# A pre-norm linear-attention and FFN kernel on one core: three loads on another queue, the FFN weights' loads placed between the rows of reciprocal loads instead of among them, and a hand-written order laid out anew

## The chip, the core and the metric

The kernel runs on one core of a Trainium2 chip. A time is that of one execution on the device, in microseconds (us). Engine names: PE is TensorE (matmuls; PEld its weight loads), DVE is VectorE, ACT is ScalarE, POOL is GpSimd, SP is SyncE, which here issues nearly all DMAs.

## The reference

All data are bf16. One batch of 2048 tokens, width 512, FFN width 1792.

```python
def _A_ref(x, wqkv, wo):                      # 32 heads of 16
    q, k, v = qkv[0], qkv[1], qkv[2]          # x @ wqkv, split by head
    phi = lambda t: jnp.where(t > 0, t + 1, jnp.exp(t)) + 1e-6
    pq, pk = phi(q), phi(k)
    kv = jnp.einsum("bhsd,bhse->bhde", pk, v)
    z = jnp.einsum("bhsd->bhd", pk)
    num = jnp.einsum("bhqd,bhde->bhqe", pq, kv)
    den = jnp.einsum("bhqd,bhd->bhq", pq, z)[..., None] + 1e-6
    o = num / den
    return o.transpose(0, 2, 1, 3).reshape(B, S, D) @ wo

h = x + _A_ref(_layernorm(x), A_wqkv, A_wo)
h2 = h + jnp.maximum(_layernorm(h) @ B_w1, 0) @ B_w2
```

## The kernel before

The 2048 tokens are 16 tiles of 128 rows, in 4 chunks of 4 tiles. The whole program is one list of words, `ORDER`. A word such as `K.7.3` calls `op_K(7, 3)`, and the words are emitted from first to last (L540 to L542). Each engine runs its own instructions in the order of its words, and waits where a word needs another engine's result, a DMA's data, or a buffer that is still being read. So the order between words of different engines means nothing, but the order within one engine, and within SP's queue, means everything. Numbers behind a name are tiles, chunks, rows and PSUM banks (there are 8 banks, all written by hand); the last number of a `T`, `K`, `Q`, `h`, `p` or `f` word without a split is the bank.

**Loads.** `lx` (L213, SP) and `ax` (L216, ACT's queue) load tiles of x: `lx.4.2` loads tiles 4 and 5. `lk`, `lq`, `lv`, `lo`, `l1`, `l2` (L219, SP) load the weights of keys, queries, values, attention output, and the FFN's w1 and w2. `l1` and `l2` come in two halves of 0.9 MB each.

**Attention, part 1, by tile.** `warm` runs matmuls on zeros. `S`, `A` (L233, L234, DVE): mean and variance; `R` (L239, ACT): reciprocal deviation; `N` (L247, DVE): normalized tile. The normalized tile is transposed by `T` (PE, L272) with `E` (ACT, L282) for tiles 0 to 4, by `X` (DMA transpose, L293, issued by SP) for the others. `K` (L301) gives the keys of a tile, `Q` (L309) the queries of a chunk, transposed. phi is built by `F` and `U` (ACT: exp and relu), `M` and `D` (DVE: min and add), and with a q ahead of the name (`qF`, `qU`, `qM`, `qD`) for queries. `G` (L353) sums phi(k)^T times the normalized rows in banks 4 to 7; `za`, `zf`, `zhi`, `zlo`, `z` sum phi(k).

**Attention, part 2.** `gA`, `gD` (L391, L394) evict G; `kv`, `kx`, `m` (L399, L407, L411) and `mA` or `mD` (ACT L414, DVE L417) form one 512x512 matrix that holds kv and wo. `d4` (L425) gives the denominators of a chunk, `dl4` and `dx4` (ACT) their reciprocals by Ln and Exp. `wb` (L453) writes these 128x512 values to DRAM; eight `rb` words (L456) read them back, each row set broadcast over 16 partitions, into `rr`, of which there is one for all chunks. `dm` (L469, DVE) multiplies phi(q) by `rr` into `pqs`; `h` (L478, PE) multiplies by the matrix, a tile at a time, and `hD` (L484, DVE) adds x.

**FFN.** `s`, `a` (L235, L236), `n` (DVE, L255) or `nA` (ACT, L261), and a transpose `x` (L294, by SP) or `t` and `v` (PE, DVE) prepare a tile; `r` (ACT) gives the reciprocal deviation of four tiles. `p` (L493; `ph` for half a chunk, L502) is the first FFN matmul of a chunk, 14 row blocks; two blocks at a time are evicted with relu by `pA` (ACT, L508) or `pD` (DVE, L513). `f` (L522) is the second, by tile, in two runs of 7 matmuls; `fo` (DVE, L530) scales and adds h, `fd` (L537, SP) stores. Tile 15 is done in three pieces of 256, 128 and 128 columns.

Two facts that the steps below use: the words `rb.1.*` of the eight rows of chunk 1 have `l2.7.7` between them in SP's queue, and `wb.0` is followed by `l1.0.2` before the eight `rb.0.*`.

Of the kernel before, what the change touches and what calls it, by code (L numbers as in the profile page):

```python
# [43 lines left out]
pD.1.2.2 n.8 a.14 fd.1 s.12 p.1.5.1 p.1.4.0 pA.1.0.2 fo.2 hD.15 s.15 n.9 pD.1.4.2 a.12 p.1.6.4 p.1.8.2 p.1.7.5
pD.1.6.2 x.10 p.1.10.6 p.1.9.3 p.1.12.4 p.1.11.7 pA.1.8.2 r.4.4 f.5.2.0.7 p.1.13.5 pD.1.12.2 fd.0 x.9 x.8
p.2.10.3 p.2.1.1 p.2.0.0 fd.3 fd.2 p.2.12.4 p.2.13.5 pA.2.0.2 pA.2.12.2 nA.12 pD.1.10.2 a.15 h.13.6 hD.13 n.15
f.7.0.0.7 s.13 a.13 p.2.3.7 p.2.11.4 f.7.0.7.7 pD.2.10.2 f.5.2.7.7 fo.5 nA.14 x.14 nA.13 p.2.2.6 pD.2.2.2 fo.7
f.4.4.0.7 f.6.7.0.7 f.6.7.7.7 p.2.4.5 x.15 p.2.8.0 p.2.5.6 pA.2.4.2 fo.6 x.12 x.13 p.3.7.3 p.2.9.1 f.4.4.7.7
# [524 lines left out]
```

## Time and profile before

| what | value |
|---|---|
| median of 3 runs | 170.41 us (170.07 to 170.49) |
| the profiled execution's own time | 169.75 us |
| its span, first to last instruction | 168.03 us |
| granted TensorE clock | 1.000 |
| last landing of a store | 167.09 us in the span |
| DMA, mean | 95 GB/s, 16.01 MB |

In a line of a timeline the columns are start, duration (both us), engine, line, operation, output<-inputs, count, and in brackets the engine's idle time before it with what ended it. In the chain of work that ended last, they are start, duration and what. In a group, busy time, mean duration in ns, and idle time before. In the page's second part each character is one of 40 slices of 4.2 us, in tenths of busy time. DMA issue lines have the count, KB of one, and the median us from issue to landing. "Matmul, start to start" is the distance between the starts of two neighbours in the trace, since busy times of matmuls overlap.

### The profile page before, as it was taken

The page shows a single profiled execution, that of the slowest core. Times are in us where ns is not written, and L with a number is a line of the kernel's source. Part 1 is how long each engine was busy: PE and PEld are TensorE (multiplying, and loading weights), DVE is VectorE, ACT ScalarE, POOL GpSimd, SP SyncE. Part 2 cuts the span into 40 slices and gives each one's busy share as a digit, 9 for nine tenths or more (in the row PEclk, how much of TensorE's full clock was granted, in tenths as well). Part 3 has the DMA queues.
Part 4 walks back from the last instruction along what each step waited for, and adds up shares of the span by engine and source line. Part 5 has one row for each costly group of instructions (what it writes and reads, how often), then busy time and mean ns, then how long its engine had stood idle before and what let it go on. Part 6 is the DMA issues. An engine that isn't in the chain of part 4 may idle for free.

```text
...
## 1 busy us (share of the span) xinstructions
PE 163.1 (97%) x924; PEld 79.6 (47%) x924; DVE 98.5 (59%) x198; ACT 67.3 (40%) x104; POOL 4.7 (3%) x21
## 2 busy tenths in 40 slices
PE   7899999999999998999999999999999999999993
...
DVE  2999999941659876428799880544415170043133
...
PEclk9999999999999999999999999999999999999999
...
DMA packets 25003, 16.01 MB, mean 95 GB/s; under 512 B 15008, under 2 KB 23968, under 8 KB 24992
## 3 DMA queue, kind: packets, MB, share of 16 engines
...
q8 instruction: 7, 0.11, 0.3%
q14 instruction: 4, 0.03, 0.1%
...
## 4 chain that ended last, share of the span: by engine, by line
PE 85%; DVE 5%; DMA 5%; SPq 2%; issue 1%; DVEq 0%
PE bk L522 29%; PE bk L493 24%; PE bk L301 8%; PE bk L353 8%; PE bk L478 7%; PE bk L309 6%; DMA rr<-scr 3%; SPq L456 2%; DMA x_nat<-in_A_x_dram 2%; DVE st L235 1%; DVE h_nat L484 1%; DVE st L233 1%; PE bk L272 1%; PE bk L377 1%; PE bk L399 1%
## 5 line engine op out<-in xcount | busy, mean ns | idle before, releaser
L522 PE MATMUL bk<-w_sb,at 128*128 128x512 bf16 (+2 forms) x252 | 50.7, 355 | 0.0
L493 PE MATMUL bk<-lnT,w_sb 128*128 128x512 bf16 x208 | 47.3, 379 | 0.0
L508 ACT ACTIVATE at<-bk 128x1024 bf16<-128x1024 f32 x15 | 14.8, 1024 | 53.1 <-PE bk L493 51.2
L522 PEld LDWEIGHTS <-at 128*128 128x128 bf16 x252 | 23.6, 98 | 25.2
L493 PEld LDWEIGHTS <-w_sb 128*128 128x128 bf16 x208 | 20.4, 98 | 24.1
L530 DVE SCALAR_TENSOR_TENSOR gT<-bk,rstd,h_nat 128x512 bf16<-128x512 f32 (+2 forms) x18 | 12.3, 687 | 23.8 <-PE bk L522 19.3
L513 DVE TENSOR_SCALAR at<-bk 128x1024 bf16<-128x1024 f32 x13 | 15.8, 1223 | 17.4 <-PE bk L493 17.2
L319 ACT ACTIVATE eb<-bk 128x1024 bf16<-128x1024 f32 (+1 forms) x18 | 16.6, 934 | 1.5 <-PE bk L309 1.0
L322 ACT ACTIVATE rb<-bk 128x1024 bf16<-128x1024 f32 (+1 forms) x18 | 16.8, 931 | 0.7 <-PE bk L301 0.7
L478 PE MATMUL bk<-m_sb,pqs 128*128 128x512 bf16 x64 | 15.8, 379 | 0.4 <-DVE pqs L469 0.4
L301 PE MATMUL bk<-wk_sb,lnT 128*128 128x512 bf16 x64 | 15.6, 379 | 0.0
L309 PE MATMUL bk<-lnT,wq_sb 128*128 128x512 bf16 x64 | 15.6, 379 | 0.0
L484 DVE TENSOR_TENSOR h_nat<-bk,x_nat 128x512 bf16<-128x512 f32 x16 | 10.8, 681 | 7.5 <-PE bk L478 7.4
L353 PE MATMUL bk<-at,h_nat 128*128 128x512 bf16 x56 | 13.2, 379 | 0.0
L233 DVE BATCH_NORM_STATS2 st<-x_nat 128x6 f32<-128x512 bf16 x16 | 10.5, 674 | 2.4 <-DMA x_nat<-in_A_x_dram 2.4
L235 DVE BATCH_NORM_STATS2 st<-h_nat 128x6 f32<-128x512 bf16 x16 | 10.9, 687 | 0.3
L478 PEld LDWEIGHTS <-pqs 128*128 128x128 bf16 x64 | 6.1, 98 | 8.3 <-DVE pqs L469 0.9
L309 PEld LDWEIGHTS <-wq_sb 128*128 128x128 bf16 x64 | 6.2, 98 | 7.3
L353 PEld LDWEIGHTS <-h_nat 128*128 128x128 bf16 x64 | 6.1, 98 | 7.3 <-issue 0.2
L301 PEld LDWEIGHTS <-lnT 128*128 128x128 bf16 x64 | 5.9, 98 | 6.6 <-DMA lnT<-h_nat 0.9
L261 ACT ACTIVATE hn<-h_nat,mv 128x512 bf16<-128x512 bf16 x7 | 4.8, 717 | 10.3 <-DVE mv L236 10.3
L469 DVE TENSOR_TENSOR pqs<-pqT,rr 128x1024 bf16<-128x1024 bf16 x8 | 5.2, 687 | 6.0 <-DMA rr<-scr 5.9
...
## 6 DMA issues: line engine op xcount, KB each, us to landing
...
out_dram<-gT SPq DMA_DIRECT2D x15, 128.0 KB, 1.9
...
```

Source lines behind the costliest of these rows:

```text
L235: op_s = lambda t: nc.vector.bn_stats(out=st2[:, t, :], in_=h_nat[:, t, :])
L301: nc.tensor.matmul(bk[:, b, :], lhsT=lnT[c][:, kd, j * P : (j + 1) * P], rhs=wk_sb[:, kd, :], start=(kd == 0), stop=(kd == KD - 1),)
L309: nc.tensor.matmul(bk[:, b, :], lhsT=wq_sb[:, kd, j * P : (j + 1) * P], rhs=lnT[c][:, kd, :], start=(kd == 0), stop=(kd == KD - 1),)
L319: nc.scalar.activation(out=buf(eb, kind, i, n), in_=bank(at_bank[kind, i], n), func=ACT.Exp)
L322: nc.scalar.activation(out=buf(rb, kind, i, n), in_=bank(at_bank[kind, i], n), func=ACT.Relu)
L353: nc.tensor.matmul(bk[:, KD + kd, :], lhsT=ln_nat[:, t, kd * P : (kd + 1) * P], rhs=pk(t)[:, 0, :], start=(not stated), stop=(len(stated) ...
L478: nc.tensor.matmul(bk[:, b, :], lhsT=pqs[:, (c * KD + jb) % NQ, j * P : (j + 1) * P], rhs=m_sb[:, jb, :], start=(jb == 0), stop=(jb == KD ...
L484: nc.vector.tensor_tensor(out=h_nat[:, t : t + n, :], in0=bank(at_bank["h", t], n), in1=x_nat[:, t : t + n, :], op=ALU.add,)
L493: nc.tensor.matmul(bk[:, b, :], lhsT=w1_sb[:, kd, f * P : (f + 1) * P], rhs=lnT[c][:, kd, :], start=(kd == 0), stop=(kd == KD - 1),)
L508: nc.scalar.activation(out=acts[c % 2][:, f : f + n, :], in_=bank(at_bank["p", c, f], n), func=ACT.Relu, scale=-1.0)
L513: nc.vector.tensor_scalar(out=acts[c % 2][:, f : f + n, :], in0=bank(at_bank["p", c, f], n), scalar1=-1.0, scalar2=0.0, op0=ALU.mult, op1= ...
L522: nc.tensor.matmul(bk[:, b, 0 : w * P], lhsT=acts[c % 2][:, f, j * P : (j + 1) * P], rhs=w2_sb[:, f, k * P : (k + w) * P], start=(f == 0), ...
```

## The change

Only `ORDER` changes. Tile 0 of x is loaded by ACT's queue ahead of tiles 1 and 2, as `ax.0.1`, so that SP's first load is that of the keys' weight. The loads of `l1` and `l2` stand between the groups of `rb` words: `l1.0.2` ahead of `wb.0`, `l1.2.2` and `l2.0.7` behind the rows of chunk 0, `l2.7.7` behind those of chunk 1. Thirteen evictions of `p` go from ACT (`pA`, 15 to 2) to DVE (`pD`, 13 to 26), five `nA` become `n` (9 to 14) with one other exchange of that kind, one `mA` becomes `mD`, and `gA` and `gD` change places. PSUM banks, and the order of nearly all words from the first K on, are new; the chunk 1 words `h.4` to `h.7` come ahead of most `p.0` words, and chunk 3's `p` words ahead of part of chunk 2's. The matmuls are the same ones.

The diff, cut to the words up to chunk 2's first stage and to the end:

```diff
 ORDER = """
-lx.0.1 ax.1.1 ax.2.1 table const masks warm.70.7.64 warm.2.7 S.0 A.0 lk.0.4 S.1 R.0.1 N.0.0.2 A.1 S.2 R.1.1
-N.0.2.2 lx.3.1 A.2 T.0.0.0.2 E.0.0.2 R.2.1 lx.4.2 N.1 S.3 T.0.4.2.2 N.2 lx.6.2 K.0.6.0.2 T.1.5 A.3 lq.0.4
-E.0.2.2 E.1 R.3.1 K.0.6.2.2 T.2.7 E.2 S.5 N.3 K.1.5.0.2 K.1.5.2.2 S.4 A.5 A.4 T.3.3 K.2.2.0.2 K.2.2.2.2 F.0.1
-S.6 E.3 Q.0.3.1 R.4.2 M.0.1 lx.8.4 lx.12.4 N.4 T.4.7 S.7 U.1.1 F.1.1 U.0.1 K.3.0.0.2 N.5 F.2.1 Q.0.1.4 K.3.0.2.2
-A.7 A.6 R.6.2 E.4 Q.0.0.3 S.10 U.2.1 F.3.1 D.0.1 N.6 M.1.1 X.5 U.3.1 A.10 N.7 D.1.1 S.9 K.4.6 qF.0.0.2 qU.0.0.2
-K.5.7 Q.0.2.0 X.6 S.8 S.13 M.2.1 A.9 S.12 X.7 S.11 A.12 M.3.1 A.13 A.8 A.11 D.3.1 F.4.2 U.4.2 R.8.2 D.2.1 K.6.2
-M.4.2 R.12.2 K.7.3 qU.0.2.2 G.0 N.9 R.10.2 U.6.2 lo.2.2 N.8 D.4.2 G.3 G.1 G.4 G.2 X.9 X.8 F.6.2 S.14 N.11 N.13
-N.12 S.15 qM.0.0.2 M.6.2 qD.0.0.2 A.15 G.5 K.9.3 K.8.2 D.6.2 qF.0.2.2 N.10 A.14 za.4.1 qM.0.2.2 X.13 G.7 X.12
-K.12.0 K.13.1 R.14.2 F.8.2 U.8.2 N.14 U.12.2 N.15 M.8.2 X.11 F.12.2 K.11.3 X.10 K.10.2 G.6 za.6.0 D.8.2 X.14
-K.14.0 X.15 qD.0.2.2 K.15.1 F.10.2 U.10.2 Q.1.1.3 l1.2.2 za.8.0 M.12.2 G.9 M.10.2 F.14.2 zf D.10.2 zhi D.12.2
-U.14.2 M.14.2 zlo G.10 G.8 D.14.2 z.1.2 z.0.2 z.2.2 z.3.2 zc lv.2.2 zh G.14 d4.0.1 dl4.0 dx4.0 G.11 G.15 G.13
-lo.0.2 lv.0.2 G.12 l2.0.7 Q.1.0.2 Q.1.3.1 gA.0.2 qF.1.0.2 gD.2.2 kv.3.7 kv.1.7 qU.1.0.2 wb.0 l1.0.2 kv.0.7
-kv.2.7 kx Q.1.2.0 rb.0.6 Q.2.1.5 qF.1.2.2 rb.0.3 rb.0.2 qM.1.0.2 m.0.2 rb.0.5 m.3.7 m.2.6 m.1.3 Q.2.0.4 qU.1.2.2
-Q.2.3.1 rb.0.4 mA.2.2 qD.1.0.2 qM.1.2.2 Q.2.2.0 rb.0.7 rb.0.1 qD.1.2.2 rb.0.0 dm.0.2.2 dm.0.0.2 mA.0.2 qU.2.0.2
-qF.2.0.2 h.1.3 d4.1.2 dl4.1 hD.1 dx4.1 wb.1 s.1 h.0.6 a.1 hD.0 s.0 Q.3.0.4 a.0 n.0 h.2.7 hD.2 nA.1 Q.3.1.5 s.2
-a.2 qU.2.2.2 qF.2.2.2 x.1 h.3.3 hD.3 Q.3.2.6 Q.3.3.7 n.2 s.3 qU.3.0.2 a.3 x.0 t.2.3 qF.3.0.2 r.0.4 n.3
-ph.0.0.2.0 ph.0.2.0.0 rb.1.2 rb.1.3 v.2 t.3.4 qU.3.2.2 rb.1.0 ph.0.3.1.0 rb.1.5 v.3 qM.2.2.2 ph.0.1.3.0 rb.1.6
-l2.7.7 rb.1.4 ph.0.2.0.1 qF.3.2.2 ph.0.3.1.1 qM.2.0.2 qM.3.0.2 qD.2.0.2 p.0.8.4 p.0.9.5 rb.1.1 pA.0.2.2 qD.2.2.2
-qM.3.2.2 qD.3.0.2 qD.3.2.2 ph.0.0.2.1 ph.0.1.3.1 rb.1.7 dm.1.2.2 pA.0.0.2 pA.0.8.2 p.0.6.0 p.0.7.1 p.0.5.3
-d4.2.5.2 dm.1.0.2 h.4.2 h.5.4 dl4.2 dl4.3 dx4.3 dx4.2 wb.2 pD.0.6.2 rb.2.0 hD.4 h.6.5 p.0.11.7 p.0.10.6 rb.2.2
-hD.6 s.6 h.7.0 hD.7 rb.2.5 p.0.4.2 p.0.13.1 p.0.12.0 pA.0.4.2 rb.2.7 pA.0.10.2 s.7 rb.2.1 rb.2.3 pA.0.12.2
-rb.2.4 f.2.2.0.7 rb.2.6 dm.2.0.2 dm.2.2.2 s.4 a.6 wb.3 a.7 f.1.3.0.7 f.3.6.0.7 rb.3.4 rb.3.0 n.6 hD.5 x.6
...
-f.12.3.0.7 f.12.3.7.7 fo.9 fo.8 r.12.4 fd.8 fd.9 f.15.5.0.14.0.2 f.13.2.0.7 fo.12 fd.12 fd.11 f.14.7.0.7
-f.14.7.7.7 fd.10 fo.15.0.2 fo.14 fd.15.0.2 fd.14 f.13.2.7.7 fo.13 fd.13 f.15.5.0.14.2.1 fo.15.2.1 fd.15.2.1
-f.15.1.0.14.3.1 fo.15.3.1 fd.15.3.1
+ax.0.1 ax.1.1 ax.2.1 table const masks warm.70.7.64 warm.2.7 S.0 A.0 S.1 R.0.1 N.0.0.2 A.1 S.2 lk.0.4 R.1.1
+T.0.1.0.2 E.0.0.2 N.0.2.2 A.2 R.2.1 N.1 lx.3.1 S.3 T.0.4.2.2 K.0.1.0.2 E.0.2.2 T.1.0 N.2 lx.4.2 lx.6.2 K.0.1.2.2
+A.3 T.2.3 E.1 R.3.1 S.5 K.1.4.0.2 K.1.4.2.2 E.2 N.3 F.0.1 S.4 lq.0.4 lx.8.4 T.3.5 A.5 E.3 A.4 K.2.7.0.2
+K.2.7.2.2 S.6 S.7 R.4.2 Q.0.1.3 U.0.1 F.1.1 N.4 lx.12.4 U.1.1 K.3.6.0.2 A.6 N.5 A.7 M.1.1 T.4.0 M.0.1 S.9 R.6.2
+N.6 F.2.1 X.5 A.9 X.6 D.1.1 D.0.1 M.2.1 K.3.6.2.2 N.7 E.4 Q.0.3.1 S.10 S.11 U.3.1 F.3.1 Q.0.0.2 A.10 S.12 K.4.4
+A.11 qU.0.0.2 qF.0.0.2 S.13 A.12 K.5.5 F.4.2 M.3.1 U.4.2 U.2.1 S.8 A.13 D.3.1 A.8 X.7 R.8.2 Q.0.2.0 K.6.2 R.12.2
+R.10.2 K.7.3 M.4.2 D.2.1 N.9 N.8 F.6.2 X.9 G.0 S.14 N.13 U.6.2 A.14 G.3 G.1 D.4.2 qF.0.2.2 S.15 M.6.2 A.15 X.8
+N.12 G.2 G.4 N.10 N.11 qM.0.0.2 qM.0.2.2 qD.0.0.2 R.14.2 G.5 K.9.3 X.13 N.15 N.14 K.8.2 qU.0.2.2 F.8.2 K.13.1
+X.12 K.12.0 D.6.2 U.8.2 F.12.2 X.11 X.10 G.6 za.4.1 K.11.3 X.14 K.10.2 X.15 M.8.2 qD.0.2.2 G.7 za.6.0 M.12.2
+U.12.2 K.14.0 D.8.2 F.10.2 lv.2.2 U.10.2 K.15.1 F.14.2 lv.0.2 D.12.2 za.8.0 lo.0.2 M.10.2 G.8 Q.1.1.3 G.9 zf
+D.10.2 zhi G.10 U.14.2 M.14.2 zlo lo.2.2 l1.0.2 D.14.2 z.3.2 z.1.2 z.2.2 z.0.2 zc zh G.14 d4.0.1 G.11 G.12 dl4.0
+dx4.0 wb.0 rb.0.1 G.15 G.13 Q.1.0.2 Q.1.3.1 gA.2.2 gD.0.2 kv.2.5 kv.3.5 kv.0.5 kv.1.5 qF.1.0.2 qM.1.0.2 Q.1.2.0
+kx qU.1.0.2 qD.1.0.2 qF.1.2.2 Q.2.0.4 qU.1.2.2 rb.0.6 rb.0.5 rb.0.0 qM.1.2.2 m.2.6 m.3.7 m.1.3 m.0.2 rb.0.7
+mD.2.2 Q.2.1.5 rb.0.4 rb.0.3 rb.0.2 Q.2.3.1 mA.0.2 qF.2.0.2 qU.2.0.2 dm.0.0.2 dm.0.2.2 l1.2.2 qM.2.0.2 qD.1.2.2
+Q.2.2.0 qU.2.2.2 h.1.3 d4.1.5 hD.1 s.1 a.1 h.0.6 h.3.4 hD.0 s.0 dl4.1 dx4.1 a.0 nA.1 l2.0.7 hD.3 wb.1 h.2.2
+qF.2.2.2 nA.0 hD.2 s.3 s.2 Q.3.3.7 a.3 x.1 Q.3.2.6 a.2 Q.3.1.5 qF.3.2.2 x.0 Q.3.0.4 n.3 n.2 t.3.0 r.0.4 qU.3.2.2
+t.2.3 qM.3.2.2 qM.2.2.2 v.3 ph.0.3.1.0 ph.0.0.2.0 ph.0.2.0.0 v.2 ph.0.3.1.1 rb.1.7 rb.1.6 ph.0.1.3.0 ph.0.1.3.1
+ph.0.2.0.1 qF.3.0.2 qD.3.2.2 qD.2.0.2 qM.3.0.2 p.0.11.7 qU.3.0.2 qD.2.2.2 rb.1.0 rb.1.1 qD.3.0.2 pD.0.2.2
+d4.2.4.2 ph.0.0.2.1 rb.1.4 rb.1.3 dl4.2 rb.1.5 rb.1.2 p.0.10.6 dm.1.0.2 dm.1.2.2 h.7.1 h.4.0 pD.0.0.2 pD.0.10.2
+hD.4 hD.7 h.5.3 h.6.2 s.4 p.0.8.0 dl4.3 dx4.2 p.0.9.1 dx4.3 s.7 l2.7.7 wb.2 pA.0.8.2 hD.5 p.0.5.5 rb.2.1 rb.2.7
+a.7 a.4 hD.6 s.5 s.6 rb.2.4 p.0.4.4 a.5 a.6 n.7 rb.2.2 rb.2.0 rb.2.3 p.0.7.2 p.0.6.1 p.0.13.7 rb.2.6 rb.2.5
+p.0.12.6 pD.0.4.2 dm.2.0.2 dm.2.2.2 r.4.4 wb.3 rb.3.4 rb.3.0 n.4 pA.0.6.2 n.5 n.6 pD.0.12.2 h.10.5 hD.10 x.6
+rb.3.2 h.9.4 hD.9 s.10 h.8.0 hD.8 h.11.7 hD.11 s.9 a.10 s.8 s.11 a.8 a.9 f.0.1.0.7 f.1.3.0.7 rb.3.7 a.11 n.10
...
+p.3.2.5 p.3.3.6 pD.3.0.2 pD.3.2.2 p.3.12.0 p.3.13.1 pD.3.12.2 p.2.11.7 f.15.5.0.14.2.1 fo.15.2.1 fd.15.2.1
+f.15.4.0.14.0.2 fo.15.0.2 p.2.7.3 p.2.6.2 fd.5 p.2.10.6 pD.2.6.2 pD.2.10.2 f.8.1.0.7 f.8.1.7.7 fo.8 fd.8
+f.9.4.0.7 f.9.4.7.7 fo.9 f.13.7.0.7 f.14.2.0.7 f.13.7.7.7 fd.9 fo.13 f.14.2.7.7 fd.15.0.2 fo.14 fd.14 f.11.7.0.7
+f.11.7.7.7 fo.11 fd.13 f.10.1.0.7 f.10.1.7.7 fo.10 fd.10 fd.11 f.12.3.0.7 f.12.3.7.7 fo.12 fd.12 f.15.0.0.14.3.1
+fo.15.3.1 fd.15.3.1
 """
```

More of the change, by code (lines that the diff above doesn't have):

```diff
@@ L39 @@
-hD.6 s.6 h.7.0 hD.7 rb.2.5 p.0.4.2 p.0.13.1 p.0.12.0 pA.0.4.2 rb.2.7 pA.0.10.2 s.7 rb.2.1 rb.2.3 pA.0.12.2
-rb.2.4 f.2.2.0.7 rb.2.6 dm.2.0.2 dm.2.2.2 s.4 a.6 wb.3 a.7 f.1.3.0.7 f.3.6.0.7 rb.3.4 rb.3.0 n.6 hD.5 x.6
-f.1.3.7.7 h.11.1 a.4 n.4 hD.11 s.11 rb.3.7 a.11 h.10.0 h.9.4 hD.9 hD.10 rb.3.3 rb.3.5 rb.3.1 rb.3.6 f.0.7.0.7
-h.8.5 f.3.6.7.7 f.0.7.7.7 s.10 a.10 rb.3.2 s.5 a.5 dm.3.0.2 fo.1 dm.3.2.2 h.12.0 hD.8 fo.3 hD.12 n.11 s.8 nA.7
-x.7 s.9 f.2.2.7.7 a.8 nA.5 x.5 x.4 nA.10 fo.0 a.9 h.14.5 hD.14 p.1.0.3 p.1.2.0 p.1.3.1 s.14 x.11 h.15.6 p.1.1.4
@@ L44 @@
[L44 to L48, printed above, removed]
@@ L49 @@
-pD.2.8.2 p.2.7.1 r.8.4 p.2.6.0 fo.4 pD.2.6.2 p.3.11.5 p.3.13.7 p.3.5.1 f.11.4.0.7 p.3.12.6 f.11.4.7.7 p.3.4.0
-pD.3.12.2 fd.4 fd.7 fd.5 fd.6 p.3.1.7 p.3.0.6 fo.11 p.3.10.4 pA.3.0.2 pA.3.10.2 pD.3.4.2 p.3.6.2 p.3.2.6 p.3.8.0
-f.10.4.0.7 p.3.9.1 pA.3.6.2 f.9.5.0.7 f.10.4.7.7 f.8.2.0.7 p.3.3.7 fo.10 f.8.2.7.7 pD.3.2.2 f.9.5.7.7 pA.3.8.2
-f.12.3.0.7 f.12.3.7.7 fo.9 fo.8 r.12.4 fd.8 fd.9 f.15.5.0.14.0.2 f.13.2.0.7 fo.12 fd.12 fd.11 f.14.7.0.7
-f.14.7.7.7 fd.10 fo.15.0.2 fo.14 fd.15.0.2 fd.14 f.13.2.7.7 fo.13 fd.13 f.15.5.0.14.2.1 fo.15.2.1 fd.15.2.1
@@ new lines @@
+a.7 a.4 hD.6 s.5 s.6 rb.2.4 p.0.4.4 a.5 a.6 n.7 rb.2.2 rb.2.0 rb.2.3 p.0.7.2 p.0.6.1 p.0.13.7 rb.2.6 rb.2.5
+p.0.12.6 pD.0.4.2 dm.2.0.2 dm.2.2.2 r.4.4 wb.3 rb.3.4 rb.3.0 n.4 pA.0.6.2 n.5 n.6 pD.0.12.2 h.10.5 hD.10 x.6
+rb.3.2 h.9.4 hD.9 s.10 h.8.0 hD.8 h.11.7 hD.11 s.9 a.10 s.8 s.11 a.8 a.9 f.0.1.0.7 f.1.3.0.7 rb.3.7 a.11 n.10
+n.8 n.9 rb.3.5 rb.3.1 rb.3.6 rb.3.3 dm.3.0.2 dm.3.2.2 n.11 f.0.1.7.7 fo.0 f.1.3.7.7 x.7 h.13.6 h.14.0 x.5 x.4
+x.11 fo.1 hD.13 s.13 hD.14 h.15.1 a.13 hD.15 h.12.7 fd.0 n.13 hD.12 s.14 f.3.2.0.7 s.12 f.3.2.7.7 p.1.13.7
@@ new lines @@
+p.1.12.6 p.1.10.0 p.1.11.1 x.10 a.14 p.1.9.3 s.15 a.12 x.9 x.8 a.15 n.12 n.14 fo.3 n.15 fd.1 pD.1.12.2 pD.1.10.2
+p.1.8.2 pD.1.8.2 p.1.1.5 x.14 p.1.0.4 p.1.3.7 pD.1.0.2 p.1.2.6 p.1.5.4 p.1.4.3 pD.1.2.2 p.1.6.5 p.1.7.6 r.8.4
+pD.1.4.2 p.2.0.3 p.2.1.4 f.2.7.0.7 pD.1.6.2 p.2.2.0 p.2.3.1 pD.2.0.2 f.2.7.7.7 pD.2.2.2 p.2.12.2 p.2.13.3 fo.2
+x.15 p.2.5.1 p.2.4.0 f.4.4.0.7 f.4.4.7.7 p.2.9.6 p.2.8.5 pD.2.12.2 r.12.4 fd.2 fd.3 pD.2.4.2 fo.4 f.5.1.0.7
+f.5.1.7.7 f.6.2.0.7 x.12 x.13 pD.2.8.2 fo.5 f.6.2.7.7 fo.6 fd.6 f.7.0.0.7 f.7.0.7.7 fo.7 fd.7 p.3.10.6 p.3.11.7
```

1 line of the change is left out of this document (added).

## The prediction

> **What bounds the kernel now.** I read the page's busy shares and its 40 slices first, then the groups.
>
> ```profile
> PE 163.1 (97%) x924; PEld 79.6 (47%) x924; DVE 98.5 (59%) x198; ACT 67.3 (40%) x104; POOL 4.7 (3%) x21
> PE   7899999999999998999999999999999999999993
> DVE  2999999941659876428799880544415170043133
> PEclk9999999999999999999999999999999999999999
> ...
> L522 PE MATMUL bk<-w_sb,at 128*128 128x512 bf16 (+2 forms) x252 | 50.7, 355 | 0.0
> L493 PE MATMUL bk<-lnT,w_sb 128*128 128x512 bf16 x208 | 47.3, 379 | 0.0
> ```
>
> TensorE is busy in every slice at a full clock, and its big groups have no idle time. Busy matmuls overlap, so I took start-to-start distances from the trace: 0.216 us for a 128x512 matmul, again and again, from 8.1 us to the end. The order changes no matmul and no tile size, so this stream is fixed. Only places where TensorE does not stream can change. There are three: the head, one wait near 65 us, and the tail.
>
> The head: the first tile of x arrives at 3.62 us and starts a chain through VectorE, ScalarE and TensorE.
>
> ```profile
> x_nat<-in_A_x_dram ACTq DMA_DIRECT2D x1, 128.0 KB, 2.6
> x_nat<-in_A_x_dram SPq DMA_DIRECT2D x1, 128.0 KB, 2.8
> ```
> ```profile
> 3.65 0.69 DVE L233 BATCH_NORM_STATS2 st<-x_nat 128x6 f32<-128x512 bf16 x1 [2.40 <-DMA x_nat<-in_A_x_dram]
> ```
>
> The first two lines are the DMA issues up to 1.2 us: tile 1 from ScalarE's queue and tile 0 from SyncE's, both issued at 0.80. The timeline line shows VectorE waiting for tile 0.
>
> The wait, in the chain of work that ended last (start, us, what) and in TensorE's timeline:
>
> ```profile
> 58.56 0.04 issue
> 58.61 0.42 SPq L456
> ...
> 59.08 5.23 DMA rr<-scr
> 64.30 0.02 issue
> 64.33 0.04 DVE pqs L469
> 64.36 0.57 issue
> 64.93 0.70 DVE pqs L469
> 65.63 0.04 issue
> 65.68 2.76 PE bk L478 x12
> ```
> ```profile
> 64.61 0.61 PE L425 MATMUL bk<-pqT,zhd 128*32 128x512 bf16 x8
> 65.68 0.61 PE L478 MATMUL bk<-m_sb,pqs 128*128 128x512 bf16 x2 [0.45 <-DVE pqs L469]
> ```
>
> The last rows of reciprocals (rr) took 5.23 us to land, because the 0.9 MB load l2.7.7 was issued among them at 57.53 and landed at 63.69. The other rr loads have a median of 2.7. TensorE lost only part of it: the step from the last L425 matmul to L478 took 0.826 us, against 0.322 after the two other d4 words, so **0.50 us**.
>
> **The change, part by part.** The profiled execution took 169.75 us for a span of 168.03; the median of the runs is 170.41. I add up against 169.75 and carry the difference to the median.
>
> *Head.* VectorE's and ScalarE's words keep their order up to N.3 and E.3, except that ScalarE issues three loads instead of two. A third issue of about 0.45 us moves the table load's end from 2.99 to 3.4, and ScalarE's first use is at 4.59: free, with 1 us of cover. Tile 0 now has the place tile 1 had, first in ScalarE's queue, and that landed at 3.42 against 3.62. In the packet records the starts are 1.83 us (ScalarE) and 2.29 (SyncE) for the same issue time. Tile 1 takes tile 2's old place (landed 4.21; S.1 needs it at 4.27 if all is 0.20 earlier). Tile 2 is issued near 1.70 and, at the 3.0 us that tile 2 took, lands at 4.7; S.2 needs it at 5.35. The keys' weight leads SyncE's queue; the same 0.9 MB must pass by its landing as before, so I leave it at 6.07, needed at 6.43. Tile 3 landed at 6.45, needed at 6.56. So the chain moves by **-0.20**. Bounds: it cannot gain more than 0.20, as tile 0 then waits for nothing but its own transfer in the best place shown; on the other side +0.9 (below).
>
> The Trainium skill speaks against this: the page "DMA: Bandwidth & Descriptors", section "Issuing engines are not separate DMA queues", says that loads from several issuing engines run on the same 16 DMA engines and that another engine saves only issue time. By that rule this term is about 0 and the sum 0.20 higher. The trace, with 0.20 us between two equal loads, does not agree for the first load.
>
> *From 8 to 35 us* VectorE is full (26.76 of 27.40 us busy from 8.1 on), so I compared what stands ahead of each due word. Ahead of A.8 there are now one D (0.41) and one A (0.17) more, about 0.45 with the overlap of neighbours; A.8 ends near 18.3 instead of 17.85. R.8 began at 18.26, so it and N.9, X.9 and the seven DMA transposes behind it (1.31 each in SyncE's queue) come 0.08 later. The last, X.15, landed at 30.93 for K.15 at 31.05, with nothing to spare. I charge +0.10. VectorE's work up to D.14 is the same set; D.14 ended at 34.97, and z was due at 35.37.
>
> *The weights.* The rr rows of chunk 0 lose l1.0.2 ahead of them, and were needed 0.5 us after landing: nothing. l1.2.2 and l2.0.7 (1.8 MB) go out after them at about 45. At the 3.1 to 3.3 us per 0.9 MB that the rows of these loads give, they end near 53, where only wb.1 (51.7) is in the queue, and its rows are not issued before x.0 at about 55.3. The eight rr rows of chunk 1 then follow without a weight: 7 steps of 0.48 and 2.6 to land give 61.2 instead of 64.30. So the wait goes, **-0.50**.
>
> l2.7.7 goes out behind them, near 59.3, ends near 64.6, and wb.2 (issued near 63.1) passes behind it.
>
> What is late next? Three p words (0.86 each) no longer stand ahead of the first h of chunk 1, so h.7 is due at 62.6 by adding up TensorE's words, 2.6 us earlier than h.4 was. From hD.1 (50.06, unchanged) to the end of dm.1.2, VectorE has 4 hD, 4 s, 4 a, 2 n, 3 qM, 2 v, 4 qD, 1 pD and 2 dm. By the group means that is 14.3 us; pairs that do not depend on each other overlap by about 0.085 (two qD took 1.28 where one takes 0.686), 21 such handovers, and four dependent ones cost 0.03: 12.6 to 12.8, so 62.7 to 62.9. Its first use is h.7's third matmul at 63.0. It fits by 0.1 to 0.3. Without any overlap it would end at 64.4, +1.4.
>
> *pA to pD, nA to n, mA to mD.* 13 FFN evictions move to VectorE, 1.22 us each instead of 1.02 on ScalarE, and five n's of 0.35 and one eviction of m come over: +18.8 us on an engine with 98.5 of 168. The m one runs from 46.2 to 47.4, dm.0 behind it ends at 48.65, and h.1 is due at 48.9. Between 60 and 73 they leave it no idle time: with hD, s, a, n.7 and three pD, dm.2 can begin at 71.85, the rr rows of chunk 2 land between 71.0 and 72.0 (first issue at 65.2; before, 69.30 to 75.99), and h.10's third matmul is due at 73.3 for an end at 73.15 to 73.3. Behind 73 us the bank that each p or f word overwrites is free by 0.3 us or more wherever I checked (p.1.5 and p.2.0 the closest): nothing. I charge +0.05 for this and chunk 1; the bounds are 0 and +1.4.
>
> *Tail.* The last piece is the same 14 matmuls of 128 columns and 0.35 us of VectorE. But before, two such pieces followed fo.13; now one follows fo.12. So a 128 KB store goes out 0.39 us ahead of the last 32 KB store.
>
> ```profile
> out_dram<-gT SPq DMA_DIRECT2D x1, 128.0 KB, 1.9
> out_dram<-gT SPq DMA_DIRECT2D x2, 32.0 KB, 1.6
> ```
>
> Of these issues after 164 us, the 32 KB store 0.42 behind the large one took 1.68, the last one 1.47. So +0.21 to +0.23; I take **+0.22**. It cannot be below nothing.
>
> Sum: -0.20 - 0.50 + 0.10 + 0.05 + 0.22 = -0.33, so 169.42 for the profiled execution and **170.1** (170.08) for the median.
>
> **The rivals.** *The queue does not matter.* Both queues had an issue at 0.80, 5 ns apart; if SyncE's is served first, or all loads simply share, tile 0 lands at 3.62 and the head gains nothing: 170.3. For it: the tie is close. Against it: the 0.46 us between the first packets. Chance 0.2. The Trainium skill's rule above is this case.
>
> *Slower: tile 1 behind the keys' weight.* Before, 128 packets of x stood ahead of the weight in SyncE's queue; now its 512 packets are offered from the start. If the two queues are not served in turn, tile 1 waits until they have gone (they took 1.74 us in the packet records), lands near 5.3, and S.1, which stands ahead of N.0 on VectorE, starts 0.9 later than 4.47. From 0.2 us of delay on, the head's gain is lost; with +0.9 the sum is +0.77: 171.2. Against it: tile 2's packets flowed at full pace while tile 0 and the weight were in flight. Chance 0.12.
>
> *VectorE becomes the bound before h.7 or h.10.* With half the overlap lost, +0.7, 170.8; with all, 171.5. Against it: each x2 and x3 group of the timeline shows the overlap. Chance 0.1.
>
> *All margins hold and the last store is not delayed:* -0.70, 169.7. Chance 0.2.
>
> **How the numbers follow.** My forecast's chance is 0.38, with 0.25 us to either side for margins of 0.1 to 0.3 that I added up from neighbours. 0.3% (0.51 us, about what a measurement of this kernel can tell from no change) puts the lines at 169.90 and 170.92. Faster: 0.2 from the last rival and a third of the forecast's lower half and a little more, 0.33. Slower: 0.12 and about half of VectorE's case, 0.17. Same: 0.50. The range reaches from the clean case, less 0.2, to the lower part of the slow ones: 169.5 to 171.0.
>
> **What would show it.** Right: tile 0's BN statistics start at 3.45; K.1 streams from 7.95; no idle time ahead of L478 at 62 to 66, with DMA rr<-scr gone from the chain; the last store lands 1.6 to 1.7 us after its issue. Wrong: S.1 waiting for x_nat; TensorE waiting for DMA lnT<-h_nat at 26 to 31 us, or for DVE pqs at 63 or 73; pD words that start late and hold a bank.

## The result, and the profile after

The changed kernel takes **172.39 us** (median of four runs, 171.26 to 172.57), the kernel before 170.24 on the same chip: a ratio of **1.0136**, interval 1.0109 to 1.0162. The forecast was 170.1, with a range up to 171.0, and the chain of reasons that led there is wrong at its first term. The profiled execution took 172.52 us for a span of 170.81, against 168.03 before: 2.78 us more. All ratios leave out executions in a slower state, among them one of 610 us, the only one of e10 with a trace, and one of 350 us (e13).

The page of the changed kernel, its busy shares and slices (4.27 us each):

```profile
PE 162.7 (95%) x908; PEld 80.1 (47%) x924; DVE 115.0 (67%) x217; ACT 50.5 (30%) x85; POOL 4.8 (3%) x21
...
PE   7399999999999999999999999999999999999992
...
DVE  2689999981388999999999766563316673621312
...
PEclk9879999999999999999999999999999999999999
```

VectorE is 16.5 us busier (98.5 before), and yet TensorE stands at 9 in every slice from the third to the last but one. So the loss is looked for in the first slices: TensorE is at 3 in the second, and the granted clock at 8 and 7 in the second and third.

The timeline from 4 to 12 us (start, duration, engine, line, what, idle time before), first two lines of the kernel before, tile 1's statistics and the first two matmuls of 512 columns, then the changed kernel:

```profile
4.47 0.66 DVE L233 BATCH_NORM_STATS2 st<-x_nat 128x6 f32<-128x512 bf16 x1
...
6.63 0.59 PE L301 MATMUL bk<-wk_sb,lnT 128*128 128x512 bf16 x2
```
```profile
5.81 0.69 DVE L233 BATCH_NORM_STATS2 st<-x_nat 128x6 f32<-128x512 bf16 x1 [1.33 <-DMA x_nat<-in_A_x_dram]
...
6.81 0.28 PE L272 MATMUL bk<-ident,h_nat 128*128 128x128 bf16 x2 [2.05 <-DVE h_nat L247]
...
8.11 1.06 PE L301 MATMUL bk<-wk_sb,lnT 128*128 128x512 bf16 x2
```

The statistics of **tile 1** start at 5.81 (4.47 before): VectorE waits 1.33 us for its data. Behind it on VectorE stand N.0 and all that follows, so TensorE idles for 2.05 us, and two matmuls of 512 columns then take 1.06 us, where the same pair took 0.59 before. The windows view says why (stretch, its length, busy time of PE, PEld, DVE, ACT and POOL, clock, DMA share, GB/s):

```profile
0.00:11.00 11.00, 7.07 (x89) 5.41 (x91) 5.50 (x19) 4.40 (x13) 4.75 (x21) 0.84 0.81 279
63.00:78.00 15.00, 14.90 (x76) 6.70 (x76) 15.00 (x27) 4.86 (x8) 0.00 (x0) 1.00 0.41 129
```

The clock records hold one stretch of 3.41 us, from 7.31 to 10.73, at half the clock; matmuls of 512 columns are 0.427 us apart there instead of 0.216. Of the four runs, the one with the full clock throughout took 171.26, the others 172.3 to 172.6: the half clock is not there in every execution, and costs about 1.1 us where it is.

The chain of work that ended last in the changed kernel (start, duration, what):

```profile
1.73 5.17 DMA x_nat<-in_A_x_dram
...
16.73 3.57 DMA lnT<-h_nat
20.35 1.04 PE bk L301 x4
...
63.92 0.55 PE bk L425 x8
64.46 0.54 PE bk L502 x4
65.01 0.05 issue
65.06 0.81 PE bk L493 x3
65.87 0.22 PE bk L478
```

The first piece is tile 2's load, issued at 1.73 and landed at 6.89: its statistics (6.92) stand right behind the work on tile 1 and wait 0.08 us more. X.7, a transposing DMA, takes 3.57 us, where 2.46 is the rule in this kernel, and K.7 starts 0.57 us late. Near 65 us all pieces are TensorE's: the wait for the last rows of reciprocals is gone.

By start-to-start distances, the span's 2.78 us are: T.0.4 later by 1.41 (7.92 against 6.51), from there to K.1 (10.67 against 8.14) another 1.12 at the half clock, K.7's wait +0.57, the wait near 65 us -0.50, the tail +0.17. They add up to 2.77.

### The profile page after: what moved, and what is told of

Same layout as the page of the kernel before. It is cut to its first block, busy times and chain, and to the rows that moved or that the text cites. A ratio compares the mean times of both kernels' runs of the same rounds, so it can differ in the third digit from the quotient of the medians.

```text
span 170.8 us, 2396 instructions
## 1 busy us (share of the span) xinstructions
PE 162.7 (95%) x908; PEld 80.1 (47%) x924; DVE 115.0 (67%) x217; ACT 50.5 (30%) x85; POOL 4.8 (3%) x21
## 4 chain that ended last, share of the span: by engine, by line
PE 87%; DMA 5%; DVE 3%; ACT 2%; issue 1%; ACTq 1%
PE bk L522 28%; PE bk L493 26%; PE bk L478 8%; PE bk L353 8%; PE bk L309 6%; PE bk L301 6%; DMA x_nat<-in_A_x_dram 3%; PE bk L502 2%; DMA lnT<-h_nat 2%; PE bk L272 1%; DVE st L233 1%; PE bk L425 1%; ACT lnT L282 1%; DVE gT L530 1%; ACT eb L319 1%
## 5 line engine op out<-in xcount | busy, mean ns | idle before, releaser
L522 PE MATMUL bk<-w_sb,at 128*128 128x512 bf16 (+2 forms) x249 | 49.6, 355 | 0.2
L493 PE MATMUL bk<-lnT,w_sb 128*128 128x512 bf16 x202 | 45.7, 379 | 0.3
L513 DVE TENSOR_SCALAR at<-bk 128x1024 bf16<-128x1024 f32 x26 | 31.5, 1223 | 13.6 <-PE bk L493 12.7
L319 ACT ACTIVATE eb<-bk 128x1024 bf16<-128x1024 f32 (+1 forms) x18 | 16.6, 931 | 4.7 <-remote 2.0
L301 PE MATMUL bk<-wk_sb,lnT 128*128 128x512 bf16 x62 | 16.6, 396 | 0.5 <-DMA lnT<-h_nat 0.4
L322 ACT ACTIVATE rb<-bk 128x1024 bf16<-128x1024 f32 (+1 forms) x18 | 16.6, 939 | 0.0
L309 PE MATMUL bk<-lnT,wq_sb 128*128 128x512 bf16 x62 | 15.0, 379 | 0.1
L478 PE MATMUL bk<-m_sb,pqs 128*128 128x512 bf16 x63 | 14.6, 379 | 0.1
L239 ACT ACTIVATE rstd<-mv,eps 128x2 f32<-128x2 f32 (+2 forms) x14 | 4.2, 299 | 20.4 <-DVE mv L236 17.3
L478 PEld LDWEIGHTS <-pqs 128*128 128x128 bf16 x64 | 6.2, 98 | 7.5 <-issue 0.2
L326 DVE TENSOR_SCALAR eb<-eb 128x1024 bf16<-128x1024 bf16 (+1 forms) x18 | 6.8, 390 | 2.1 <-ACT eb L319 2.0
L247 DVE TENSOR_SCALAR h_nat<-x_nat,mv,rstd 128x512 bf16<-128x512 bf16 (+1 forms) x17 | 6.4, 394 | 0.8 <-ACT rstd L240 0.8
```

The lines of the kernel that those rows point to most:

```text
L301: nc.tensor.matmul(bk[:, b, :], lhsT=lnT[c][:, kd, j * P : (j + 1) * P], rhs=wk_sb[:, kd, :], start=(kd == 0), stop=(kd == KD - 1),)
L309: nc.tensor.matmul(bk[:, b, :], lhsT=wq_sb[:, kd, j * P : (j + 1) * P], rhs=lnT[c][:, kd, :], start=(kd == 0), stop=(kd == KD - 1),)
L319: nc.scalar.activation(out=buf(eb, kind, i, n), in_=bank(at_bank[kind, i], n), func=ACT.Exp)
L322: nc.scalar.activation(out=buf(rb, kind, i, n), in_=bank(at_bank[kind, i], n), func=ACT.Relu)
L478: nc.tensor.matmul(bk[:, b, :], lhsT=pqs[:, (c * KD + jb) % NQ, j * P : (j + 1) * P], rhs=m_sb[:, jb, :], start=(jb == 0), stop=(jb == KD ...
L493: nc.tensor.matmul(bk[:, b, :], lhsT=w1_sb[:, kd, f * P : (f + 1) * P], rhs=lnT[c][:, kd, :], start=(kd == 0), stop=(kd == KD - 1),)
```

## The experiments

Ratios are against the kernel before on the same chip, with 95% intervals; spans and instants are of one profiled execution.

### The head: tile 1 behind the keys' weight

**e3**, the new head alone on the kernel before:

```diff
-lx.0.1 ax.1.1 ax.2.1 table
+ax.0.1 ax.1.1 ax.2.1 table
```

> The kernel before with only the new head (tile 0 from ScalarE's queue, so the keys' weight leads SyncE's). If the head alone makes the loss: tile 1 lands near 5.8, TensorE's first K streams 1.3 later, or 2.5 later if it falls to half clock, and since the wait near 65 us stays: 171.6 to 172.8. If the loss needs the new order, 170.2 to 170.9.

Ratio 1.0127 (1.0087 to 1.0167). Tile 1 landed at 5.62, its statistics started at 5.64, and the half clock came from 7.48 to 10.90. This one word makes a loss as large as the whole change's. X.7 took 2.45 here.

**e1**, the change with the old head:

```diff
-ax.0.1 ax.1.1 ax.2.1 table
+lx.0.1 ax.1.1 ax.2.1 table
```

> The new order with the head of before: tile 0 first in SyncE's queue, then the keys' weight; tiles 1 and 2 from ScalarE's. If the whole loss comes from the head (tile 1 behind the weight, and the half clock after it), what is left is my sum without the head: -0.50 for the wait, +0.17 for the tail, so 169.7 to 170.1, faster than before by 0.2% and within 0.3%; tile 1 lands near 4.2 and the first BN statistics follow each other as before. If the rest of the order costs too (the wait of 0.57 us for the DMA transpose of tile 7, full VectorE), it stays at 170.5 or above.

Ratio 1.0030 (1.0009 to 1.0051), span 168.46, full clock. The rest of the change is thus no gain either. Its terms: K.1 0.30 later (8.44 against 8.14), because tile 2 was served behind the weight and landed at 5.79 instead of 4.21; K.7 0.48 later; the wait near 65 us -0.50; the tail +0.18. Sum 0.46, measured 0.43.

Tile 2's race with the weight is a matter of some 25 ns. In the kernel before, tile 2's issue on ScalarE ran from 1.217 to 1.672 and the weight's on SyncE from 1.255 to 1.696. In e1 tile 2's ran from 1.226 to 1.695 and the weight's from 1.253 to 1.671: it started first again, but ended second. In the traces with this pair, tile 2 is early where its issue ends first (4.21 in the kernel before, 3.96 in e7) and late where the weight's does (5.25 to 5.80 in e1, e5, e6 and e14). So a part of e1's 0.30 us can be how this race fell in the executions that were traced; how it falls in the others is not recorded.

**e2**, the keys' weight in four loads:

```diff
-lk.0.4
+lk.0.1 lk.1.1 lk.2.1 lk.3.1
```

> The changed kernel with the keys' weight loaded by four DMAs of 128 rows of 1 KB instead of one of 512, in the same place of the same queue: same bytes. If the DMAs of both queues get their descriptors made in turn, in a time that grows with their number (0.46 us for 128 in the trace of before), tile 1 is served behind the first quarter: first packet near 2.8, landed by 4.2 to 4.5, no wait of S.1 over 0.1, full clock, and 169.5 to 169.9. If tile 1 was late because it shares the DMA engines with the weight's 512 KB, nothing changes: tile 1 lands near 5.8, 172.3.

Ratio 1.0087 (1.0060 to 1.0114). VectorE's timeline of this kernel:

```profile
3.62 0.69 DVE L233 BATCH_NORM_STATS2 st<-x_nat 128x6 f32<-128x512 bf16 x1 [2.38 <-DMA x_nat<-in_A_x_dram]
...
4.45 0.66 DVE L233 BATCH_NORM_STATS2 st<-x_nat 128x6 f32<-128x512 bf16 x1
```

The second statistics follow at 4.45 with no wait, as before the change: tile 1 landed at 4.24, behind one quarter of the weight instead of the whole. So tile 1 waits for the transfer that stands ahead of it in the other queue, and not for all bytes of the weight; a plain sharing of bandwidth would have left tile 1 late. The time, 170.79 us, is still above the 169.5 to 169.9 expected: the three added issues put the queries' weight back (issued 4.46, landed 10.78), and TensorE waits for that instead.

**e4**, the warm-up matmuls longer, to keep TensorE busy until tile 1 is there:

```diff
-warm.70.7.64
+warm.108.7.64
```

> The changed kernel with 108 warm-up matmuls instead of 70, which fills TensorE's idle time until tile 1 is there; nothing else. If the half clock between about 7.3 and 10.7 us comes from that idle time, the first K matmuls are 0.216 apart and the time falls by 1.1 to 171.2 in every run, with tile 1 as late as in the changed kernel. If the half clock has another cause, it stays at 172.3.

Ratio 1.0181 (1.0161 to 1.0202). The clock stayed full and K.1 began at 9.53 instead of 10.67, though T.0 itself, behind the added matmuls, began at 7.26 instead of 6.81. So the idle time is what halves the clock. The gain of 1.14 us at K.1 was lost again. An instruction packet of 16 KB at 28.2 us fell into X.10 and X.14 (3.93 and 3.30 us; a step of 1009 ns in place of 216): 0.79. The rows of chunk 0 came late, as two of their issues took 1.03 and 1.56 us of SyncE instead of some 0.43; h.1, and d4.1 behind VectorE's work on these rows, lose 1.08 us by it. The span is 0.65 us above the changed kernel's. Why the two issues took so long is open.

**e8** and **e9** ask what the turn goes by. In e8, 512 KB in 128 long rows stand between the two queues' first transfers; in e9, 32 KB in 512 short rows do:

```diff
-... lk.0.4
+... lx.12.4 lk.0.4        # e8
+... ls lk.0.4             # e9: dma x_nat[:, 12:16, 0:32] <- x
```

> The changed kernel with another transfer put between tile 0 and tile 1: ahead of the keys' weight (512 KB in 512 rows of 1 KB) SyncE now issues tiles 12 to 15 of x (512 KB in 128 rows of 4 KB each, or as many as the trace shows). The keys' weight is later for it, so the time is no readout; what is read is tile 1, issued by ScalarE just behind. Theory A (each queue's transfer is turned into descriptors in turn, about 0.46 us for each 128): tile 1's first packet comes at about 2.8 us instead of 4.47, and it has landed by 4.6 us if there is room for its packets, instead of 5.79. Theory B (tile 1 waits for the bytes ahead of it, 512 KB in both): its first packet comes at 4.2 us or later and it lands at 5.5 us or later.

> The changed kernel with one more transfer in SyncE's queue just ahead of the keys' weight: 512 rows of only 64 bytes (32 KB in all) out of tiles 12 to 15 of x, into places that the real load of these tiles overwrites later. The keys' weight itself is later for it, so the time is no readout; what is read is tile 1, issued by ScalarE behind tile 0. Theory A (the two queues' transfers are turned into packets in turn, each for a time that goes with its number of rows, about 0.46 us for 128): tile 1's first packet comes at about 4.4 us, as behind the keys' weight (4.47), and it lands at 5.5 us or later. Theory B (tile 1 waits for the bytes ahead of it): 32 KB are a quarter of a tile, so its first packet comes by 3.0 us and it lands by 4.6 us.

e8: tile 1's first packet came near 4.2 us and it landed at 5.30, between the two expectations; tile 0 was itself slow (4.59), as its packets of 1 KB took turns with packets of 4 KB. It does not decide. e9: the first packet came at about 2.8, the landing at 4.07. So the number of rows alone is not what counts, and **my theory A is wrong**; bytes fit both. They do not fit all: in e9 tile 2's packets began about 1.1 us behind the weight's first, with some 155 of the weight's 512 gone, where tile 1 in the changed kernel waited 2.1 us, until about 400 had gone. What exactly the turn goes by stays open.

e9 is a mend too, since its extra transfer moves the weight's issue from 0.80 to 1.54, behind tile 1's (1.20). **e15** times it:

> The kernel of e9 once more, timed: the changed kernel with a transfer of 512 rows of 64 bytes between tile 0 and tile 1 on the one side and the keys' weight on the other, which moves the weight's issue from 0.80 to 1.54 us, behind tile 1's (1.20). In one look the statistics of tile 1 started at 4.10 us instead of 5.81, the clock was 1.0 throughout, X.7 still took 3.33 us, and the time was 170.30. Theory (tile 1's place behind the weight, and the half clock that follows from the idle time, are what makes the change slower than its old head): ratio 1.003 to 1.005 against the kernel before, as e1 (1.0030), where the change has 1.0136. Rival (the one look was a chance, since the clock varies between executions): ratio 1.008 or more.

VectorE's timeline of e15:

```profile
4.39 0.69 DVE L236 BATCH_NORM_STATS2 st<-x_nat 128x6 f32<-128x512 bf16 x1 [0.52 <-DMA x_nat<-in_A_x_dram]
...
5.70 0.69 DVE L236 BATCH_NORM_STATS2 st<-x_nat 128x6 f32<-128x512 bf16 x1 [0.28 <-DMA x_nat<-in_A_x_dram]
```

Ratio 1.0052 (1.0029 to 1.0075), span 168.55, full clock, with the loads of x still on ScalarE: near e1's, as the theory said, and below the rival's 1.008. Putting the weight's issue 0.74 us later takes 2.26 us off the changed kernel's span.

### K.7: an instruction packet in a transposing DMA

The page lists two queues of instruction packets beside the data. One of 8 KB fell into X.7 in the changed kernel, e1, e2 and e4 (at 18.8, 16.6, 16.5 and 17.7 us), and X.7 took 3.3 to 3.6 us in each; in the kernel before it came at 19.1, and in e3 at 21.7, between two transposing DMAs, and X.7 took 2.46. e1's DMA window over X.7 (queue: packets, MB, share; then the issue with its us to landing) and TensorE's timeline:

```profile
q1 hardware_dynamic: 1069, 0.26, 39.2%
q14 instruction: 1, 0.01, 0.6%
...
lnT<-h_nat SPq DMA_TRANSPOSE x1, 3.3
```
```profile
18.01 1.04 PE L301 MATMUL bk<-wk_sb,lnT 128*128 128x512 bf16 x4 [0.32 <-DMA lnT<-h_nat]
```

**e5** and **e6** ask whose instructions these are: e1 with 14 more short VectorE instructions, or 7 more of ScalarE's, ahead of `masks`:

```diff
-table const masks
+table const pv.14 masks   # e5: vector.memset(eps6, 1e-6), 14 times
+table const pc.7 masks    # e6: scalar.activation(Copy) of 128x1, 7 times
```

> The kernel of e1 (the change with tile 0 issued by SyncE) with 14 more short VectorE instructions (memsets of a constant that is there already) near the start. In e1 a packet of an instruction queue (8 KB) comes at 16.6 us, in the middle of X.7, the transposing DMA whose landing K.7 waits for; 46 to 47 VectorE instructions had started before it, against 57 in the kernel before, where it fell at 19.1 us between two transposing DMAs. Theory A (the packet is VectorE's code, fetched after a fixed number of its instructions): 14 instructions at the start bring it forward to 11 to 12.5 us, X.7 takes about 2.46 us again, the step of K.7 falls from 697 to about 216 ns, and the time falls by some 0.45 us, to about 1.000 of the kernel before or a little under (169.3 to 169.6 where the kernel before takes 169.35). Theory B (the packet is ScalarE's, or comes at a fixed point for another reason): the packet stays at 16 to 17 us, X.7 takes 3.3 us, and the time stays at about 1.003.

> The kernel of e1 with 7 more short ScalarE instructions (copies of one element per partition into a buffer that is written later) near the start. Theory B (the packet of 8 KB at 16.6 us is ScalarE's code): 33 to 34 ScalarE instructions had started before it, so 7 more bring it forward by some 3 us, to 13 to 14.5 us; X.7 then takes 2.46 us, the step of K.7 falls to 216 ns, and the time falls by some 0.45 us unless an earlier transposing DMA is hit. Theory A (it is VectorE's): the packet stays at 16 to 17 us, X.7 takes 3.3 us, and the time is that of e1, about 1.003 of the kernel before.

e5: the packet came at 13.0 us; e6: still at 16.6. It is **VectorE's**. The time did not fall as theory A said (1.0015, 1.0000 to 1.0030, against e6's 1.0018, 1.0002 to 1.0035): the packet now fell into X.5 (3.48 us) and X.6 (2.71), and K.5 waited instead of K.7, a step of 766 ns.

```profile
15.21 1.04 PE L305 MATMUL bk<-wk_sb,lnT 128*128 128x512 bf16 x4 [0.39 <-DMA lnT<-h_nat]
```

In e6 a second 8 KB packet moved from 43.9 to 29.2 us, into X.14 (3.19 us): that one is ScalarE's. Counted in the traces, VectorE had started 60 or 61 instructions at its packet in every kernel with the old order, and 50 in the changed kernel, e1 and the other kernels with the new order and the same memsets (the 57 and 46 to 47 of e5's expectation are counted too low); 54 with e5's 14 more. So it is not a plain count of instructions: the 14 added ones brought it forward by 10 of the others.

**e10** used 32 of these memsets, **e11** also put tile 3 of x ahead of the keys' weight:

```diff
-table const masks ... lk.0.4
+table const pv.32 masks ... lk.0.4          # e10
+table const pv.32 masks ... lx.3.1 lk.0.4   # e11
```

> The kernel of e5 with 32 instead of 14 short VectorE instructions near the start. With 14 the packet of the instruction queue moved from 16.6 to 13.0 us, where it delayed X.5 and X.6 instead of X.7 (step of K.5 766 ns), and the time stayed. Theory A (the packet is VectorE's code, and what costs about 0.5 us is only that it falls into a transposing DMA that the path waits for): with 32 it comes at 10 to 11 us, ahead of X.5; X.5, X.6 and X.7 each take 2.46 to 2.57 us, no step of K.5 to K.7 is over 430 ns, and the time falls by some 0.45 us against e5, to a ratio of 0.998 to 1.000. Rival (the X chain is late for another reason, such as its order behind VectorE's work): the packet moves, but a step of 600 to 800 ns stays somewhere in K.5 to K.7 and the ratio stays at 1.0015 to 1.003.

> The kernel of e10 (the change with tile 0 back on SyncE and 32 short VectorE instructions) with tile 3 of x, 128 rows, moved in SyncE's queue from behind the keys' weight to ahead of it, so that tile 2 in ScalarE's queue stands behind 128 rows and not, by a few ns of issue time, behind the weight's 512. Theory (transfers are taken in turn by rows): tile 2 lands at 4.3 us or earlier instead of 5.8, the third statistics start at 5.55 us instead of 5.81, the keys' weight lands about 0.4 us later (6.1 to 6.4 us) and is still in time, and the time is 0.2 to 0.3 us below e10: a ratio of 0.996 to 0.998. Rival (the weight then is what is late, or the head's order of VectorE's work gives the 0.3 us back): the ratio is that of e10 or above.

Both miss for a plain reason: a memset of this kind takes 0.127 us of VectorE, not the 0.06 I had counted on, so 32 of them end at 5.06 us and the first statistics wait for them. Ratios 1.0116 (1.0072 to 1.0159) and 1.0112 (1.0083 to 1.0142). e11's trace shows the packet at 13.1, ahead of X.5 (issued 14.89), and X.5 to X.7 at 2.45 to 2.57 us.

**e14** moves the packet the other way, by four VectorE instructions fewer:

```diff
-        nc.vector.memset(eps5[:], 1e-5)
+        nc.gpsimd.memset(eps5[:], 1e-5)      # and eps6, ones, zeros[:, P:]
```

> The kernel of e1 (the change with tile 0 issued by SyncE; ratio 1.0030 with an interval from 1.0009 to 1.0051) with four short constant memsets at the start moved from VectorE to GpSimd. In all kernels with the new order the packet of 8 KB came when VectorE had started 50 instructions (54 with 14 added ones, 62 with 32), which is at 16.6 us in e1, inside X.7 (issued 14.65, landed 17.97). Theory (it is fetched after so much of VectorE's program, and X.7 and K.7 are late by it alone): with four fewer it comes two to three instructions of the old count later, at 17.2 to 17.9 us, when X.7 has landed or nearly; X.7 takes 2.45 to 2.7 us, the step of K.7 is 216 to 350 ns instead of 697, and the time falls by 0.3 to 0.48 us: ratio 1.000 to 1.001. Rival (the late landing has another cause): the packet moves and the step of K.7 stays at about 700 ns, ratio 1.003.

The packet came at 17.40, 0.5 us behind X.7's landing. e14's DMA window over X.7, and TensorE's timeline:

```profile
q1 hardware_dynamic: 1070, 0.26, 52.0%
...
lnT<-h_nat SPq DMA_TRANSPOSE x1, 2.5
```
```profile
16.47 1.89 PE L301 MATMUL bk<-wk_sb,lnT 128*128 128x512 bf16 x8
```

X.7 took 2.45 us, the eight matmuls of K.6 and K.7 run without a step, and the span is 167.78 against e1's 168.46: 0.48 for K.7, and 0.20 at K.1 because tile 2 landed at 5.25 this time. Ratio **0.9986** (0.9969 to 1.0004). So the packet (0.31 us in e1, 0.47 in the changed kernel) in a transposing DMA that the path waits for is the whole of K.7's wait.

### The wait near 65 us

**e7**, the kernel before with only this load moved behind its eight rows:

```diff
-l2.7.7 rb.1.4 ... rb.1.7 dm.1.2.2
+rb.1.4 ... rb.1.7 l2.7.7 dm.1.2.2
```

> The kernel before with one operation moved: the load of the second FFN weight's last part in SyncE's queue from ahead of the eight row loads of the first chunk to behind them. Nothing else of the change. Theory A (the wait near 65 us is the row loads' queueing behind this weight, and the head is the whole of the loss): the last row load of the first chunk takes about 2.6 us instead of 3.2, the wait of 0.50 us goes, and the time falls by 0.45 to 0.50 us: ratio 0.997, about 168.9 where the kernel before takes 169.35. Rival (the wait comes from the order of VectorE's work or from other traffic, or the work saved is lost at the next chunk): no change, ratio 0.999 to 1.001.

The chain of work in e7:

```profile
64.69 0.55 PE bk L425 x8
65.23 1.83 PE bk L478 x8
```

The last row load took 2.61 us and L478 follows L425 directly; the span is 167.53, 0.50 less than before, as theory A said. The timed ratio is 0.9987 (0.9969 to 1.0006), smaller than the 0.997 expected: the mechanism is shown by the traces, the gain in the median is not.

### Looking for a kernel that beats both

**e12** and **e13** add to e7 a mend of tile 2's race with the weight, by tile 3 or by a transfer of 64 bytes ahead of the weight; **e16** adds the latter to e14:

```diff
-lk.0.4
+lx.3.1 lk.0.4   # e12
+ty lk.0.4       # e13, e16: dma x_nat[0:1, 12, 0:32] <- x
```

> The kernel before with two operations moved in SyncE's queue and nothing else: the second FFN weight's last part behind the eight row loads of the first chunk (as in e7, whose ratio was 0.9987 with an interval from 0.9969 to 1.0006), and tile 3 of x ahead of the keys' weight, which keeps tile 2 from ever standing behind the weight. Theory: no wait at 65 us and tile 2 landed by 4.3 us in every execution, 0.3 to 0.5 us less than the kernel before, ratio 0.997 to 0.9985. Rival (the wait's end is given back at the next chunk, or varies with something that these two moves do not touch): ratio 0.999 to 1.000.

> The kernel before with the second FFN weight's last part moved behind the first chunk's row loads (as in e7, ratio 0.9987 with an interval from 0.9969 to 1.0006), and with a transfer of one row of 64 bytes put in SyncE's queue between tile 0 and the keys' weight (overwritten later by the real load). It only makes the weight's issue some 0.3 to 0.4 us later, so that tile 2, issued by ScalarE at 1.22 us, is ahead of it for certain and not by 30 ns. Theory (the wait at 65 us and, in some executions, tile 2 behind the weight are what can be saved): tile 2 lands by 4.3 us, the weight by 6.5 us, no wait of K.0 over 0.3 us, ratio 0.996 to 0.998. Rival (the weight becomes late, as in e12 where it landed at 7.46): K.0 waits, ratio 1.000 or more.

> The kernel of e14 with the one-row transfer of e13 between tile 0 and the keys' weight: the change with its old head, with tile 2 ahead of the weight for certain, and with the packet behind X.7. What then differs from the kernel before on the path is the wait at 65 us that is gone (0.50 us) and the tail (0.18 us more). Theory (the terms add up): tile 2 lands by 4.3 us, the third statistics start at 5.55 us instead of 5.81, ratio 0.997 to 0.999. Rival (the packet falls back into X.7, since the head is 0.3 us earlier but the X chain with it, or the weight is late): ratio 1.000 or more.

Ratios: e12 1.0013 (0.9982 to 1.0044), e13 0.9992 (0.9968 to 1.0017), e16 0.9997 (0.9979 to 1.0015). All three are nearer to their rivals' numbers than to the theories', though each interval reaches into the theory's range. Tile 2 did land early (4.25, 4.03, 3.62), but the weight landed later: 7.46 in e12, where K.0 waits 1.05 us for it and the half clock comes in the traced execution (7.61 to 11.02; the clock was lowered in two of the twelve executions); 6.47 and 6.87 in e13 and e16, with tile 3 behind it at 6.82 and 7.22, where 6.45 was just in time. In these three heads, what one load gains the next one loses. **No version is shown to be faster than the kernel before**; e14 and e7 come nearest.

## Why the prediction was wrong, step by step

- **Head, -0.20: the step that failed.** "Tile 1 takes tile 2's old place (landed 4.21)" took the place within ScalarE's queue for the place among all loads. Tile 1 landed at 5.79, behind the 512 KB that SyncE had issued 0.45 us ahead of it, and the head cost 2.5 us, 1.4 of them by the late tile and 1.1 by the clock. The bound of +0.9 was named but too small, and the rival that had this mechanism ("tile 1 behind the keys' weight", chance 0.12) gave 171.2. I set it aside since "tile 2's packets flowed at full pace while tile 0 and the weight were in flight"; but tile 2's issue had ended 24 ns ahead of the weight's, and the weight's packets came behind it. The row showed the order, not a sharing; e1, where the order of these two turned, shows the reverse.
- **The gain of 0.20 in the same term was no property of ScalarE's queue.** It rested on tile 1's landing at 3.42 against tile 0's at 3.62, whose issues ended at 1.189 and 1.200. In e12, with the same first three loads, they ended at 1.200 (ScalarE) and 1.198, in e14 at 1.198 and 1.188, and tile 0 landed first both times (3.31 against 3.49, and 3.58 against 3.74). With the new head tile 0 landed at 3.00 to 3.60 (changed kernel, e2, e3, e4), with the old one at 3.31 to 3.66 (the kernel before, e1, e5, e7, e12, e14): a gain is not shown.
- **The clock, not in the sum at all.** TensorE's idle time of 2.05 us costs another 1.1 us by the half clock, in the executions that have it. Any rival that adds idle time ahead of the stream should have had this price.
- **8 to 35 us, +0.10: the wrong place.** I looked at X.15, whose margin held. The loss came at X.7, from an instruction packet that a different number of VectorE instructions moves: +0.57 (+0.48 in e1). It stands in the page's queue list, and I did not look at when its packets come.
- **The wait near 65 us, -0.50: right**, in its mechanism and size. The last row load took 2.63 us, and e7 gets the same from this one move.
- **VectorE's margins, +0.05: nothing measured, which is within the bounds of 0 and +1.4.** From 63 to 78 us it is busy 15.00 of 15.00 us, and no step of TensorE there waits for it.
- **Tail, +0.22: right**, measured +0.17; 0.12 of it is the last store, 1.59 us to landing instead of 1.47. The DMA issues of the changed kernel after 160 us (KB, us to landing):

```profile
out_dram<-gT SPq DMA_DIRECT2D x3, 128.0 KB, 1.9
out_dram<-gT SPq DMA_DIRECT2D x1, 32.0 KB, 1.6
```

The Trainium skill's rule that I had weighed, that loads from several engines share the same DMA engines and another engine saves only issue time ("DMA: Bandwidth & Descriptors", section "Issuing engines are not separate DMA queues"), fits tile 0, for which no gain is shown. It does not say what decided here: that the order of issue across the queues sets who waits (tile 1 at 5.79 or at 4.37, changed kernel and e15).
